# Ordering the first batch of an attention and mixer kernel by hand

## The chip, the cores and the metric

The kernel runs on one core of one Trainium2 chip. The time is device microseconds of one execution; medians of several executions are quoted. An execution counts as disturbed only when it is over 1.5% above the fastest of the same kernel. A trace and its page come from one execution with the profiler on, so a page shows one case of what varies between executions.

Names used below: PE is TensorE's matmuls, PEld its weight loads, DVE VectorE, ACT ScalarE, POOL GpSimd, SP SyncE. `SPq`, `ACTq`, `POOLq` mark what an engine's sequencer does, such as issuing a transfer.

## The reference

Eight batches; per batch twelve heads of cosine attention (448 rows, 64 columns), then a low-rank mixing over the rows, then two channel matmuls with a relu between, plus residual.

```python
q_n = q / (norm(q) + 1e-6);  k_n = k / (norm(k) + 1e-6)
attn = softmax(q_n @ k_n.T / tau)
x = concat_heads(attn @ v)                      # (8, 448, 768)
u = x + (x.T @ U @ V).T                         # rank 32, over the 448 rows
out = u + relu(u @ w_ch1) @ w_ch2               # 768 -> 3072 -> 768
```

## The kernel before

Heads are worked in pairs, six pairs to a batch, and pairs are loaded and normalised in groups (1, 1, 2, 2 pairs in the first batch, then 2, 2, 2). For a group: squares of queries and keys, their sums (`reduce`), a root on ScalarE (`root`), the inverse, and the scaling. For a pair: `step_T` transposes on TensorE and copies the result, `step_S` makes the scores and their exponentials, `step_V` the attention output in two halves, `step_A` and `step_H` the mixing, which ends in a copy into `u`. From the second batch on, TensorE is filled up between these steps with the channel matmuls of the batch before (`fill`). In the first batch there are none yet. The cuts below are shortened; `...` marks what is left out, and the last list is written with short names.

```python
def square(self, j):
    ...
    if self.early:                               # early = gi < 2 : groups 0 and 1
        nc.scalar.activation(sq[...], self.flat(t), AF.Square)
    else:
        nc.gpsimd.tensor_mul(sq[...], self.flat(t), self.flat(t))
...
def step_T(b, p):
    tp = psum.tile([128, 8, 128], BF, name="tp", tag="ps_x", bufs=1)
    ...                                          # eight transposes
    nc.vector.tensor_copy(out=t..., in_=tp...)   # qkT
...
def step_H(b, p):
    ...
    nc.vector.tensor_copy(out=u_of(b)[:, p, 0:S], in_=up)   # up: bank ps_x too
...
for n in range(NPAIR + 1):                       # one order for all batches (short names)
    parts = [S(n, 0, 1), V(n-1, 0), S(n, 2, 3), V(n-1, 1), T(n+1), A(n-1), H(n-1)]
    ...                                          # with shares of fill between
```

## Time and profile before

| | before |
|---|---|
| median time | 648.8 us |
| span of the profiled execution | 646.9 us |
| PE busy | 94% |
| first transposes | 13.06 us |
| first channel matmul | 62.43 us |
| TensorE full from | 64.6 us to 642.4 us |

The prediction below shows the page, the stretches and the chain; here is only how to read them. A row of digits has forty slices of 16 us, a 9 is a slice at least nine tenths busy. TensorE's row is full from the fifth slice, so this kernel can gain only in the first 65 us. One view is added here: stretches of the kernel before around its one clock dip. The columns are the stretch, its length, busy us and count of PE, PEld, DVE, ACT and POOL, the granted clock, the DMA share and GB/s.

```profile
46.00:49.60 3.60, 1.84 (x27) 1.15 (x23) 3.49 (x8) 1.15 (x4) 2.34 (x3) 1.00 1.15 234
49.60:56.50 6.90, 5.96 (x56) 3.83 (x52) 4.47 (x9) 3.32 (x5) 6.90 (x6) 0.51 1.14 231
```

TensorE was busy for half of the 3.6 us, and its granted clock is at half for the 6.9 us after them.

### The profile page before, as it was taken

The numbers are of one execution on the slowest core, as the hardware profiler recorded it, in microseconds if no ns is written. First come the engines' busy times: TensorE is split into PE (matmuls) and PEld (weight loads), VectorE is DVE, ScalarE is ACT, GpSimd is POOL, SyncE is SP. The second block draws the span as 40 slices with busy tenths as digits, with TensorE's granted clock in tenths as the row PEclk, the third lists the DMA queues.
The fourth block names the chain that finished last, engine by engine and source line by source line (L and its number), as shares of the span: only waits on it lengthen the run. The fifth ranks groups of instructions, "written<-read, shape, count | busy, mean of one in ns | idle before, by whom it ended". The sixth has DMA issues, their size and how long they took to land.

```text
span 646.9 us, 12173 instructions
## 1 busy us (share of the span) xinstructions
PE 609.4 (94%) x5160; PEld 360.4 (56%) x5160; DVE 273.3 (42%) x524; ACT 273.3 (42%) x501; POOL 195.2 (30%) x158
## 2 busy tenths in 40 slices
PE   1467999999999999999999999999999999999997
PEld 0244556655566556665566655665566555665564
DVE  4788335355244455364353453463442543210000
ACT  2465554345433454345433455334523454324310
POOL 7877244043141341340431431431404401000000
PEclk9997999999999999999999999999999999999999
DMA  7899991350315420161315302044311100001011
GB/s 195 196 220 234 233 241 43 98 147 4 83 35 126 110 73 16 32 168 48 86 26 135 95 24 79 25 117 105 87 25 26 50 1 1 25 25 26 1 50 49
DMA packets 51782, 54.33 MB, mean 84 GB/s; under 512 B 5552, under 2 KB 48112, under 8 KB 51728
## 3 DMA queue, kind: packets, MB, share of 16 engines
q1 hardware_dynamic: 44288, 43.14, 26.1%
q0 software_dynamic: 7120, 10.18, 8.6%
q8 instruction: 40, 0.66, 0.4%
q10 hardware_dynamic: 320, 0.23, 0.1%
q14 instruction: 14, 0.11, 0.1%
HBM read 52.02 MB, written 11.01 MB: 97 GB/s over the span
## 4 chain that ended last, share of the span: by engine, by line
PE 91%; DVE 6%; DMA 1%; ACT 0%; issue 0%; SPq 0%; ACTq 0%
PE mp L390 34%; PE mp L363 34%; PE av L309 5%; PE sc L282 5%; PE tp L260 3%; PE sc L274 2%; DVE qn L241 2%; PE av L302 2%; PE av L331 2%; DVE ss L215 1%; PE up L342 1%; PE mp L399 1%; PE up L347 1%; DVE qkT L262 1%; DVE X L316 1%; DMA kst<-in_k_dram 1%
## 5 line engine op out<-in xcount | busy, mean ns | idle before, releaser
L390 PE MATMUL mp<-w_sb,relu 128*128 128x384 bf16 x1344 | 246.8, 326 | 0.0
L390 PEld LDWEIGHTS <-relu 128*128 128x128 bf16 x1344 | 123.7, 98 | 77.9 <-issue 7.4
L241 POOL TENSOR_TENSOR kb<-kst,inv 128x512 bf16<-128x512 f32 x46 | 59.3, 1310 | 336.3 <-DVE inv L233 284.8
L363 PEld LDWEIGHTS <-w_sb 128*128 128x128 bf16 x1152 | 106.0, 98 | 92.9 <-issue 7.8
L284 ACT ACTIVATE E<-sc 128x896 bf16<-128x896 f32 x144 | 126.3, 917 | 46.3 <-PE sc L282 46.2
L367 ACT ACTIVATE relu<-mp 128x448 bf16<-128x448 f32 x156 | 84.7, 543 | 134.4 <-PE mp L363 134.4
L363 PE MATMUL mp<-uE,w_sb 128*128 128x448 bf16 x576 | 122.9, 353 | 1.1 <-DVE uE L349 1.1
L363 PE MATMUL mp<-uO,w_sb 128*128 128x448 bf16 x576 | 118.0, 353 | 0.0
L404 ACT COPY o_sb<-mp 128x384 f32<-128x384 f32 x50 | 23.9, 478 | 109.0 <-PE mp L399 109.0
L215 DVE TENSOR_REDUCE ss<-sq 128x16 f32<-128x1024 f32 (+1 forms) x50 | 58.1, 1166 | 3.3 <-ACT sq L207 3.3
L315 DVE RECIPROCAL rd<-av 128x4 f32<-128x4 f32 x96 | 17.1, 178 | 95.4 <-PE av L309 95.4
L241 DVE TENSOR_TENSOR qn<-qst,inv 128x512 bf16<-128x512 f32 x48 | 53.4, 1150 | 0.0
L282 PE MATMUL sc<-qkT 64*128 64x448 bf16 x288 | 45.5, 368 | 8.2 <-DVE qkT L262 6.1
L210 POOL TENSOR_TENSOR sq<-kst 128x1024 f32<-128x1024 f32 x23 | 52.0, 2262 | 2.7 <-DMA qst<-in_q_dram 2.7
L309 PE MATMUL av<-v,E 128*128 128x65 bf16 x1152 | 52.8, 195 | 0.0
L369 DVE TENSOR_SCALAR relu<-mp 128x448 bf16<-128x448 f32 x36 | 22.5, 625 | 67.0 <-PE mp L363 67.0
L262 DVE COPY qkT<-tp 128x1024 bf16<-128x1024 bf16 x48 | 33.0, 687 | 36.7 <-PE tp L260 36.7
L309 PEld LDWEIGHTS <-E 128*128 128x128 bf16 x1152 | 46.2, 98 | 0.0
L210 POOL TENSOR_TENSOR sq<-qst 128x1024 f32<-128x1024 f32 x23 | 43.5, 1892 | 0.0
L316 DVE TENSOR_TENSOR X<-av,rd 128x256 bf16<-128x256 f32 x96 | 40.8, 425 | 3.3
L334 ACT CAST A_sb<-av 128x128 bf16<-128x128 f32 x48 | 12.6, 263 | 61.7 <-PE av L331 61.7
L349 DVE CAST uO<-up 128x448 bf16<-128x448 f32 x24 | 14.9, 623 | 53.9 <-PE up L347 53.9
(66 smaller groups left out, 394.7 us busy)
## 6 DMA issues: line engine op xcount, KB each, us to landing
out_dram<-o_sb SPq DMA_DIRECT2D x54, 192.0 KB, 2.7
w_sb<-in_moe_w_ch_dram POOLq DMA_DIRECT2D x8, 1152.0 KB, 27.0
qst<-in_q_dram SPq DMA_DIRECT2D x23, 256.0 KB, 3.9
vst<-in_v_dram SPq DMA_DIRECT2D x46, 128.0 KB, 2.9
kst<-in_k_dram SPq DMA_DIRECT2D x44, 128.0 KB, 3.7
qst<-in_q_dram SPq DMA_DIRECT2D x23, 192.0 KB, 4.0
vst<-in_v_dram SPq DMA_DIRECT2D x46, 96.0 KB, 2.8
kst<-in_k_dram SPq DMA_DIRECT2D x44, 96.0 KB, 3.4
```

The lines of the kernel that those rows point to most:

```text
L210: nc.gpsimd.tensor_mul(sq[:, 0:self.nh * 4, :], self.flat(t), self.flat(t))
L215: nc.vector.reduce_sum(self.ss[:, j, 0:self.nh * 4], self.sq[j][:, 0:self.nh * 4, :], axis=AX.X)
L241: eng.tensor_mul(o[:, j, :, :, :], t[:, 2 * j:2 * j + 2, :, :].rearrange("p h c d -> p c h d"), iv.unsqueeze(3).to_broadcast([128, 4, 2, D]))
L262: nc.vector.tensor_copy(out=t.rearrange("p a b -> p (a b)"), in_=tp.rearrange("p a b -> p (a b)"))
L282: nc.tensor.matmul(out=sc[:, h, 0:S], lhsT=t[r, 1, c * 128:(c + 1) * 128], rhs=t[r, 0, 0:S], start=True, stop=True)
L284: nc.scalar.activation(out=e[:, 2 * c:2 * c + 2, 0:S], in_=sc[:, :, 0:S], func=AF.Exp)
L309: nc.tensor.matmul(out=av[:, i, h, :], lhsT=e[:, 2 * c + h, ic * 128:(ic + 1) * 128], rhs=vv[:, 2 * j + h, c, :], start=False, stop=(i == ...
L316: nc.vector.tensor_mul(X[:, 2 * half:2 * half + 2, :].rearrange("p i (h d) -> p i h d", h=2), av[:, :, :, 0:D], rd.rearrange("p (i h) o -> ...
L363: nc.tensor.matmul(out=mp, lhsT=w1_sb[:, cc, f * 128:(f + 1) * 128], rhs=u[:, cc, 0:S], start=(cc == 0), stop=(cc == CC - 1))
L367: nc.scalar.activation(out=relu[:, f, o:o + S], in_=mp, func=AF.Relu)
L390: nc.tensor.matmul(out=mp, lhsT=relu[:, f, r0:r0 + 128], rhs=w2_sb[:, f, half * HC:(half + 1) * HC], start=(f == 0), stop=False, skip_grou ...
L404: nc.scalar.copy(out=o[:, cols], in_=mp)
```

## The change

Its intent: the first batch has no channel matmuls to hide its waits, so its steps are written out by hand in the order in which the engines can take them, and work is moved off VectorE and GpSimd, which the first batch keeps busiest.

```diff
-        nc.gpsimd.dma_start(out=U_sb[0:64, :, 0:R], ...)       # mixer loads: POOL
+        nc.scalar.dma_start(out=V_raw, in_=moe_V)              # now ScalarE
+        nc.scalar.dma_start(out=U_raw[0:64, :, :], ...)
+        nc.scalar.dma_start(out=U_raw[64:128, 0:3, :], ...)
...
-            self.early = gi < 2
+            self.early = gi < 3                                # group 2's squares on ScalarE
...
+        if b == 0 and p < 2:                                   # qkT in halves
+            nc.scalar.copy(out=t[:, 1, :]..., in_=tp[:, 4:8, :])
+            nc.vector.tensor_copy(out=t[:, 0, :]..., in_=tp[:, 0:4, :])
...
+        if b == 0 and half == 1:                               # second half: channel bank
+            bank = psum.tile([128, 512], FP, name="mp", tag="ps_m", bufs=2)
...
+        if b == 0:
+            nc.scalar.copy(out=u_of(b)[:, p, 0:S], in_=up)     # u on ScalarE, also in ps_m
...
-    load(0, "k", nc.scalar)
-    load(0, "q", nc.sync)
+    load(0, "k", nc.sync, nc.scalar)                           # loads split over two queues
+    load(0, "q", nc.sync, nc.scalar)
...
+    A(3)                                                       # mixing one pair later
+    V(4, 0)
+    T(6)
+    Hs(3)
+    Sc(5, 2, 3)
+    V(4, 1)
+    g4.scale(0, 1, V_)
+    g4.values()
+    load_all(6)
+    load_w2(12, 24)                                            # fifth of five weight transfers
```

The hand order runs to pair 6's first scores; from there the loop with its fill goes on.

More of the change, by code (lines that the diff above doesn't have):

```diff
@@ L113 @@
     U_sb = const.tile([128, 4, 128], BF, name="U_sb")
-    V_raw = const.tile([R, S], BF, name="V_raw")
+    U_raw = const.tile([128, 4, R], FP, name="U_raw")
+    V_raw = const.tile([R, S], FP, name="V_raw")
     V_sb = const.tile([128, S], BF, name="V_sb")
@@ L123, in load_mixer @@
         nc.gpsimd.memset(U_sb, 0.0)
-        nc.gpsimd.dma_start(out=U_sb[0:64, :, 0:R],
-                            in_=moe_U[0:256].rearrange("(p c) r -> p c r", c=4))
-        nc.gpsimd.dma_start(out=U_sb[64:128, 0:3, 0:R],
-                            in_=moe_U[256:448].rearrange("(p c) r -> p c r", c=3))
         nc.gpsimd.memset(V_sb, 0.0)
-        nc.gpsimd.dma_start(out=V_raw, in_=moe_V)
+        nc.gpsimd.memset(U_raw[64:128, 3, :], 0.0)
+        nc.scalar.dma_start(out=V_raw, in_=moe_V)
+        nc.scalar.dma_start(out=U_raw[0:64, :, :], in_=moe_U[0:256].rearrange("(p c) r -> p c r", c=4))
+        nc.scalar.dma_start(out=U_raw[64:128, 0:3, :], in_=moe_U[256:448].rearrange("(p c) r -> p c r", c=3))
     def place_mixer():
@@ L134, in place_mixer @@
         body = V_sb[0:R, 0:384].rearrange("r (c p) -> r c p", p=128)
-        nc.gpsimd.tensor_copy(out=body[:, :, 0:64], in_=lo[:, 0:3, :])
-        nc.gpsimd.tensor_copy(out=body[:, :, 64:128], in_=hi)
-        nc.gpsimd.tensor_copy(out=V_sb[0:R, 384:448], in_=lo[:, 3, :])
+        nc.scalar.copy(out=U_sb[:, :, 0:R], in_=U_raw)
+        nc.scalar.copy(out=body[:, :, 0:64], in_=lo[:, 0:3, :])
+        nc.scalar.copy(out=body[:, :, 64:128], in_=hi)
+        nc.scalar.copy(out=V_sb[0:R, 384:448], in_=lo[:, 3, :])
     def load_w1(f0, f1):
@@ L159, with load @@
             group_of[(b, p0 + j)] = (gi, j)
-    def load(gi, what, eng):
+    def load(gi, what, *engs):
         b, p0, n = groups[gi]
+        engs = list(engs) * 4
         h0, nh = 2 * p0, 2 * n
@@ L174, in load @@
             allh = slice(h0, h0 + nh)
-            eng.dma_start(out=dst(qst[s], L, slice(0, nh), 4), in_=src(q, allh, 0, 256, 4))
-            eng.dma_start(out=dst(qst[s], U2, slice(0, nh), 3), in_=src(q, allh, 256, 448, 3))
+            engs[0].dma_start(out=dst(qst[s], L, slice(0, nh), 4), in_=src(q, allh, 0, 256, 4))
+            engs[1].dma_start(out=dst(qst[s], U2, slice(0, nh), 3), in_=src(q, allh, 256, 448, 3))
             return
@@ L179, in load @@
         ev, od = slice(h0, h0 + nh, 2), slice(h0 + 1, h0 + nh, 2)
-        eng.dma_start(out=dst(t, L, slice(0, nh, 2), 4), in_=src(x, ev, 0, 256, 4))
-        eng.dma_start(out=dst(t, U2, slice(0, nh, 2), 3), in_=src(x, ev, 256, 448, 3))
-        eng.dma_start(out=dst(t, L, slice(1, nh, 2), 3), in_=src(x, od, 0, 192, 3))
-        eng.dma_start(out=dst(t, U2, slice(1, nh, 2), 4), in_=src(x, od, 192, 448, 4))
+        engs[0].dma_start(out=dst(t, L, slice(0, nh, 2), 4), in_=src(x, ev, 0, 256, 4))
+        engs[1].dma_start(out=dst(t, U2, slice(0, nh, 2), 3), in_=src(x, ev, 256, 448, 3))
+        engs[2].dma_start(out=dst(t, L, slice(1, nh, 2), 3), in_=src(x, od, 0, 192, 3))
+        engs[3].dma_start(out=dst(t, U2, slice(1, nh, 2), 4), in_=src(x, od, 192, 448, 4))
     norm = {}
@@ L203, in square @@
             t = (qst, kst)[j][self.s]
-            sq = work.tile([128, NG * 4, D], FP, name="sq", tag="sq", bufs=2)
+            if self.gi < 2:
+                sq = work.tile([128, 8, D], FP, name="sq1", tag="sq1", bufs=2)
+            else:
+                sq = work.tile([128, NG * 4, D], FP, name="sq", tag="sq", bufs=2)
             self.sq[j] = sq
@@ L261, in step_T @@
         t = work.tile([128, 2, 512], BF, name="qkT", tag="qkT", bufs=3)
-        nc.vector.tensor_copy(out=t.rearrange("p a b -> p (a b)"),
-                              in_=tp.rearrange("p a b -> p (a b)"))
+        if b == 0 and p < 2:
+            nc.scalar.copy(out=t[:, 1, :].rearrange("p (c r) -> p c r", c=4), in_=tp[:, 4:8, :])
+            nc.vector.tensor_copy(out=t[:, 0, :].rearrange("p (c r) -> p c r", c=4), in_=tp[:, 0:4, :])
+        else:
+            nc.vector.tensor_copy(out=t.rearrange("p a b -> p (a b)"),
+                                  in_=tp.rearrange("p a b -> p (a b)"))
         qkT[(b, p)] = t
@@ L296, in step_V @@
         X = X_of[(b, p)]
-        bank = psum.tile([128, 512], FP, name="av", tag="ps_av", bufs=1)
+        if b == 0 and half == 1:
+            bank = psum.tile([128, 512], FP, name="mp", tag="ps_m", bufs=2)
+        else:
+            bank = psum.tile([128, 512], FP, name="av", tag="ps_av", bufs=1)
         av_of[(b, p)] = bank
@@ L337, in step_A @@
         est.act(0.3)
-        up = psum.tile([128, S], FP, name="up", tag="ps_x", bufs=1)
+        if b == 0:
+            up = psum.tile([128, S], FP, name="mp", tag="ps_m", bufs=2)
+        else:
+            up = psum.tile([128, S], FP, name="up", tag="ps_x", bufs=1)
         up_of[(b, p)] = up
@@ L348, in step_H @@
                          start=False, stop=True, skip_group_check=True)
-        nc.vector.tensor_copy(out=u_of(b)[:, p, 0:S], in_=up)
         est.pe(0.19)
-        est.dve(0.62)
+        if b == 0:
+            nc.scalar.copy(out=u_of(b)[:, p, 0:S], in_=up)
+        else:
+            nc.vector.tensor_copy(out=u_of(b)[:, p, 0:S], in_=up)
+            est.dve(0.62)
         if b % 2 == 1 and p == NP - 1:
@@ L440, in load_all, with T, Sc, V @@
                 load(gi, x, nc.sync)
-    load(0, "k", nc.scalar)
-    load(0, "q", nc.sync)
-    load(1, "q", nc.sync)
-    load(1, "k", nc.sync)
+    load(0, "k", nc.sync, nc.scalar)
+    load(0, "q", nc.sync, nc.scalar)
+    load(1, "k", nc.sync, nc.scalar)
+    load(1, "q", nc.sync, nc.scalar)
+    load(2, "k", nc.gpsimd)
+    load(2, "q", nc.sync)
     load(0, "v", nc.sync)
-    load(2, "q", nc.sync)
-    load(2, "k", nc.gpsimd)
     load(1, "v", nc.gpsimd)
+    load_mixer()
     load(2, "v", nc.sync)
-    g0, g1, g2, g3 = preps[0:4]
-    load_mixer()
+    g0, g1, g2, g3, g4 = preps[0:5]
+    V_, P_ = nc.vector, nc.gpsimd
+    def T(n):
+        step_T(*pairs[n])
+    def Sc(n, *cs):
+        step_S(*pairs[n], cs)
+    def V(n, half):
+        step_V(*pairs[n], half)
+    def A(n):
+        step_A(*pairs[n])
+    def Hs(n):
+        step_H(*pairs[n])
     g0.square(1)
     g0.square(0)
-    g1.square(1)
-    g1.square(0)
-    g2.square(1)
-    g2.square(0)
     g0.reduce(1)
@@ L463 @@
     g0.root()
+    g1.square(1)
+    g1.square(0)
     g0.invert()
-    g0.scale(1, 0, nc.vector)
-    g0.scale(0, 0, nc.vector)
-    g0.values()
-    place_mixer()
+    g0.scale(1, 0, V_)
+    g0.scale(0, 0, V_)
+    g2.square(1)
     g1.reduce(1)
-    step_T(*pairs[0])
+    T(0)
+    Sc(0, 0)
     g1.reduce(0)
     g1.root()
+    Sc(0, 1)
+    g2.square(0)
     g1.invert()
-    g1.values()
-    load_all(3)
+    g1.scale(1, 0, P_)
+    g1.scale(0, 0, V_)
+    g0.values()
+    load_all(3)
+    load_w1(0, 768)
+    T(1)
+    g2.reduce(1)
+    Sc(0, 2, 3)
+    g2.reduce(0)
+    g2.root()
+    Sc(1, 0, 1)
+    g2.invert()
+    g2.scale(1, 0, P_)
+    g2.scale(0, 0, V_)
+    g2.scale(1, 1, P_)
+    V(0, 0)
+    g1.values()
+    T(2)
+    place_mixer()
+    Sc(1, 2, 3)
+    V(0, 1)
+    g2.scale(0, 1, V_)
+    g3.square(1)
+    g3.square(0)
+    g2.values()
+    load_w1(768, 1920)
+    Sc(2, 0, 1)
+    load_all(4)
+    A(0)
+    V(1, 0)
+    T(3)
+    Hs(0)
+    Sc(2, 2, 3)
+    V(1, 1)
+    g3.reduce(1)
+    g3.reduce(0)
+    load_w1(1920, 3072)
+    Sc(3, 0)
+    g3.root()
+    Sc(3, 1)
+    g3.invert()
+    g3.scale(1, 0, P_)
+    g3.scale(0, 0, V_)
+    g3.scale(1, 1, P_)
+    A(1)
+    V(2, 0)
+    T(4)
+    g3.scale(0, 1, V_)
+    Hs(1)
+    Sc(3, 2, 3)
+    V(2, 1)
+    g3.values()
+    load_all(5)
+    g4.square(1)
+    g4.square(0)
+    Sc(4, 0, 1)
+    A(2)
+    V(3, 0)
+    T(5)
+    g4.reduce(1)
+    Hs(2)
+    Sc(4, 2, 3)
+    V(3, 1)
+    load_w2(0, 12)
+    g4.reduce(0)
+    Sc(5, 0)
+    g4.root()
+    Sc(5, 1)
+    g4.invert()
+    g4.scale(1, 0, P_)
+    g4.scale(0, 0, V_)
+    g4.scale(1, 1, P_)
+    A(3)
[8 more added lines that the diff above has]
+    load_w2(12, 24)
+    A(4)
+    V(5, 0)
+    V(5, 1)
+    Hs(4)
+    Sc(6, 0, 1)
+    A(5)
+    T(7)
+    Hs(5)
+    fill.extend(steps_m1(0) + steps_m2(0))
     after = {}
@@ L480, in put @@
         after.setdefault((n, at), []).append(fn)
-    for gi in range(1, len(groups)):
+    for gi in range(5, len(groups)):
         m, n, g = first_pair[gi], groups[gi][2], preps[gi]
         two = range(n)
-        if gi >= 3:
-            put(m - 3, 0, lambda g=g: (g.square(1), g.square(0)))
-            put(m - 3, 6, lambda g=g: g.values())
-        if gi == 2:
-            put(0, 0, lambda g=g: (g.reduce(1), g.reduce(0), g.root(), g.invert()))
-            put(0, 2, lambda g=g: ([g.scale(0, j, nc.vector) for j in two],
-                                   [g.scale(1, j, nc.gpsimd) for j in two], g.values()))
-        elif gi > 2:
-            put(m - 2, 0, lambda g=g: g.reduce(1))
-            put(m - 2, 1, lambda g=g: g.reduce(0))
-            put(m - 2, 2, lambda g=g: g.root())
-            put(m - 2, 3, lambda g=g: (g.invert(), [g.scale(1, j, nc.gpsimd) for j in two]))
-            for j in two:
-                put(m - 2, 4 + j, lambda g=g, j=j: g.scale(0, j, nc.vector))
-        if gi >= 1:
-            put(m - 1, 6, lambda gi=gi: load_all(gi + 3))
@@ L501 @@
-    put(0, -1, lambda: (g1.scale(1, 0, nc.vector), g1.scale(0, 0, nc.vector)))
-    put(1, 4, lambda: (load_w1(0, 768), load_w1(768, 1536)))
-    put(2, 4, lambda: (load_w1(1536, 2304), load_w1(2304, 3072)))
-    put(3, 4, lambda: (load_w2(0, 6), load_w2(6, 12)))
-    put(4, 4, lambda: (load_w2(12, 18), load_w2(18, 24)))
-    for n in range(NPAIR + 1):
+        put(max(m - 3, NP), 0, lambda g=g: (g.square(1), g.square(0)))
+        put(max(m - 3, NP), 6, lambda g=g: g.values())
+        put(m - 2, 0, lambda g=g: g.reduce(1))
@@ L508 @@
+        put(m - 2, 1, lambda g=g: g.reduce(0))
+        put(m - 2, 2, lambda g=g: g.root())
+        put(m - 2, 3, lambda g=g: (g.invert(), [g.scale(1, j, P_) for j in two]))
+        for j in two:
+            put(m - 2, 4 + j, lambda g=g, j=j: g.scale(0, j, V_))
+        put(m - 1, 6, lambda gi=gi: load_all(gi + 3))
+    put(NP, 6, lambda: load_all(7))
+    for n in range(NP, NPAIR + 1):
         b, p = pairs[n] if n < NPAIR else (B, 0)
-        prev = pairs[n - 1] if n > 0 else None
         now, nxt = n < NPAIR, n + 1 < NPAIR
-        parts = [
-            now and (lambda: step_S(b, p, (0, 1))),
-            prev and (lambda: step_V(*prev, 0)),
-            now and (lambda: step_S(b, p, (2, 3))),
-            prev and (lambda: step_V(*prev, 1)),
-            nxt and (lambda: step_T(*pairs[n + 1])),
-            prev and (lambda: step_A(*prev)),
-            prev and (lambda: step_H(*prev)),
-        ]
@@ L520 @@
-        weights = [w if part else 0 for part, w in zip(parts, (2, 2, 2, 2, 2, 2, 1))]
-        left = NP - p + 0.85 if p else 0.85
-        nf = len(fill) if p == 0 else int(round(len(fill) / left))
+        if n == NP:
+            parts = [None, None, lambda: Sc(n, 2, 3), None, None, None, None]
+        else:
+            parts = [
+                now and (lambda: Sc(n, 0, 1)),
+                lambda: V(n - 1, 0),
+                now and (lambda: Sc(n, 2, 3)),
+                lambda: V(n - 1, 1),
+                nxt and (lambda: T(n + 1)),
+                lambda: A(n - 1),
+                lambda: Hs(n - 1),
+            ]
@@ L523 @@
+        weights = [w if part or n == NP else 0 for part, w in zip(parts, (2, 2, 2, 2, 2, 2, 1))]
+        last = p == 0 and n > NP
+        left = NP - p + 0.85 if not last else 0.85
+        nf = len(fill) if last else int(round(len(fill) / left))
         given = acc = 0
-        for fn in after.pop((n, -1), []):
-            fn()
         for i, (fn, w) in enumerate(zip(parts, weights)):
@@ L535 @@
             given = want
-        if p == 0 and n > 0:
+        if last:
             while fill:
```

## The prediction

> **What bounds the kernel now.** I read the page first (busy shares and slices), then the stretches of the first batch, the chain that ended last, and the order of time on the engines.
>
> The page of the kernel before:
>
> ```profile
> PE 609.4 (94%) x5160; PEld 360.4 (56%) x5160; DVE 273.3 (42%) x524; ACT 273.3 (42%) x501; POOL 195.2 (30%) x158
> ...
> PE   1467999999999999999999999999999999999997
> ...
> PEclk9997999999999999999999999999999999999999
> DMA  7899991350315420161315302044311100001011
> ```
>
> From the fifth slice on TensorE is full until the tail. Only the first four slices, some 65 us, can be shortened; all later time is matmul work that the change does not touch. The stretches (us, then busy us and count of PE, PEld, DVE, ACT, POOL, then clock, DMA share, GB/s):
>
> ```profile
> 13.00:26.00 13.00, 4.09 (x23) 2.03 (x23) 11.17 (x16) 3.74 (x8) 9.24 (x9) 1.00 0.88 205
> 26.00:62.40 36.40, 26.39 (x316) 16.87 (x316) 28.35 (x56) 21.03 (x37) 28.76 (x25) 0.91 1.07 221
> ```
>
> While the first batch's attention runs, VectorE is busiest (39.5 of 49.4 us). The chain (start, length, what) agrees: it hops along VectorE's operations.
>
> ```profile
> 19.62 2.27 DVE ss L215 x2
> ...
> 23.25 2.15 DVE qn L241 x2
> ...
> 48.72 2.61 DVE qn L241 x2
> 51.33 0.54 DVE uE L349
> ...
> 64.61 0.35 PE mp L363
> ```
>
> The last line is the first channel matmul after which TensorE never waits again. So the figure to predict is when the changed kernel reaches the same state.
>
> The order of time at the start (start, us, engine; brackets: idle before):
>
> ```profile
> 3.65 0.49 ACTq L183 DMA_DIRECT2D kst<-in_k_dram  x1
> 6.99 0.63 ACT L207 ACTIVATE sq<-kst 128x512 f32<-128x512 f32 x1 [4.97 <-DMA kst<-in_k_dram]
> ...
> 9.68 0.63 ACT L207 ACTIVATE sq<-kst 128x512 f32<-128x512 f32 x1 [1.54 <-DMA kst<-in_k_dram]
> ...
> 10.73 0.20 ACT L224 ACTIVATE ss<-ss 128x16 f32<-128x16 f32 x1
> ...
> 15.59 1.89 POOL L210 TENSOR_TENSOR sq<-qst 128x1024 f32<-128x1024 f32 x1
> ...
> 16.18 1.32 DVE L231 TENSOR_SCALAR ss<-ss 128x16 f32<-128x16 f32 x1 [0.53 <-ACT ss L225]
> ```
>
> Group 0's root (10.73) stands behind group 1's squares, which wait for their load; its sums were ready at 9.1. And a VectorE operation of 0.17 us took 1.32 us: it ended at 17.50, with GpSimd's square (17.48).
>
> **What the Trainium skill says.** "SBUF — State Buffer", section "Who interferes with whom": VectorE and GpSimd share a port pair; an operation in a 2-port mode, or with two SBUF inputs, can block on the other; ScalarE never waits. The trace agrees (1.32 against 0.17 us; the query scaling took 0.68 us with GpSimd idle and 1.38 us beside its key scaling). "Trainium Kernel Development and Optimization", section "Key Constraints": issuing from several engines only saves the sequencer's issue time, the same 16 DMA engines serve all. Here an issue costs about 0.6 us, so that is what split loads can save. "TensorE: Matmul & The Clock Gate", Part 1: half clock until a window of about 3.4 us was busy. The trace agrees: four transposes took 0.61 us at 13 us and 0.38 us at 29 us, and the granted clock was 0.50 from 50 to 56 us, after two microseconds with TensorE half idle.
>
> **The change, part by part.** Durations are those of the trace above.
>
> Split loads: keys and queries of group 0 are issued in three slots per queue instead of four (one of them late, at 3.65), so group 0 lands near 5.5 us instead of 6.9. But the built order shows nine issues on ScalarE ahead of its first square, the last three for the mixer, and six of the nine carry a wait for an earlier transfer. The trace before shows eight transfers issued freely and the next waiting for a landing some 2.9 us after issue. SyncE issues group 1's first query transfer at about 4.1 us, it lands at 7.5; the mixer's last issue waits for it, 7.5 + 0.6 = 8.1. So the first square starts at 8.2, **1.2 us later** than now. The earlier root gains 1.6 us (10.73 against 9.15). Root at 10.35, first transposes at 12.7 against 13.05: only 0.4 us gained.
>
> Squares of group 2 on ScalarE: adds two of about 1.05 us there and removes 3.8 us of GpSimd; the 1.32 us block goes, and GpSimd scales group 1's keys beside VectorE. Group 2's sums, which hold up pair 1 now (19.6 to 23.25 in the chain), no longer stand before the first scaling of pair 1: its scores move from 26.1 to about 20.6, the largest single gain, 5.5 us.
>
> Evictions: six copies of u (0.62 us each) leave VectorE and become six of 0.54 us on ScalarE. Two query/key copies are halved: VectorE saves 0.3 us each, ScalarE gains 0.6 us each. Placing the mixer adds some 1.1 us to ScalarE.
>
> Mixing one pair later, and half of the attention output and u in the channel matmuls' banks: a transpose no longer waits for u's copy in its bank. Those waits are 3.0 us of TensorE in all now, but they lie on VectorE's time, not instead of it.
>
> Walking the new program order with these durations, each operation at the later of its engine being free and its inputs: scores of pair 2 start at 26.5 (31.4 now), of pair 3 at 30.7 (37.4), pair 4 at 38.5 (43.1), pair 5 at 43 (49.3), pair 6 at 52.5. VectorE then has an attention half every 2.9 us, 5.76 us a pair against 5.95 now. Its own work fell to about 4.9 us a pair (reduce 1.2, scaling 1.1, attention output 1.25, transposed copy 0.65, small ones 0.7), but it idles in each pair of groups: about 0.5 us for the round trip to ScalarE's root, and about 1.4 us for the attention output behind TensorE's transposes. ScalarE meanwhile waits 1.5 us with that root for the sums, and at the end copies pair 5's 128x128 block only after two exponentials of pair 6 (0.9 us each). That puts the last mixing at 55.1 and the first channel matmul at **55.3 us**.
>
> What compares with that: before, TensorE is full from 64.6, and its last matmul ends at 642.4. At that point it had done more than the changed kernel has at 55.3: the rest of pair 6's scores (0.59), half of pair 7's (0.48) and five channel matmuls (0.95), 2.0 us. So the equivalent time before is 62.6. Gain 62.6 - 55.3 = **7.3 us**. The tail and the 1.9 us between span and time stay. 648.8 - 7.3 = 641.5. I booked every query scaling at 1.1 us, and some of the second halves will find GpSimd idle at 0.7: I take 1 us off, **640.5 us**.
>
> Weights: no gain in itself. The DMA engines are full from 30 to 99 us now, and the eight transfers ran from issue at 31 to about 96:
>
> ```profile
> w_sb<-in_moe_w_ch_dram POOLq DMA_DIRECT2D x8, 1152.0 KB, 27.0
> ```
>
> That is 9.44 MB in 65 us, 145 GB/s. In the new order the first is issued at 19, the next two near 31, the last at 51: 1.2 MB land by 28, the other 8.3 MB 57 us after 31, at 88. The output matmuls start 36 us after the channel matmuls, at 91: 3 us to spare.
>
> **The rivals.**
>
> A: *the hand order closes most gaps.* VectorE's work from the first sum to pair 5's last output adds up to some 33 us; from 8.9 us, without any wait, that ends at 42, and channel matmuls could start near 45. For it: VectorE is the busiest engine before. Against: ScalarE has some 35 us of work from 8.2 on, equally full, and the two pass sums, roots and outputs back and forth. Half of the way would be 50: gain 12.6 us, 636.
>
> B: *the weights turn into the wait.* If the first phase shrinks a lot, output matmuls would start near 85 while the last weights land near 88 or later, since loads and weights want the same engines. That caps the gain at about 9 us: 640. For it: DMA share over 1 until 99 us. Against: fewer later groups compete by then.
>
> C: *TensorE stays at half clock.* It is full at half speed for about 6 us per pair (transposes 1.05, scores 2.0, outputs 2.1, mixing 1.2) against 3.1 at full speed. A dip or a late warm-up adds perhaps 2 to 4 us: 643 to 645. For it: the dip at 50 us now. Against: busier stretches come sooner.
>
> D: *ScalarE becomes the bound*, its blocked start and copies cancelling VectorE's relief: gain 3 us, 646.
>
> **Range and chances.** The walk carries about 4 us of error each way, mostly from waits between VectorE and ScalarE. Two per cent is 13 us, channel matmuls at 49.6; only rival A reaches it. So 634 to 646, and faster by over 2% with 0.2. Slower by 2% has no path that I see: 0.01.
>
> **What would show it.** First square at 8.2 us, after the mixer's issues; first transposes near 12.7; pair 1's scores near 20.6; no TENSOR_SCALAR of a microsecond on VectorE; first channel matmul near 55 with no TensorE wait after it; output matmuls near 91 without a wait for weights. Wrong: channel matmuls before 50 (the walk has too many waits), a wait of TensorE for a weight transfer (B), transposes at 0.6 us after 30 us (C), or ScalarE busy over 90% from 26 us on (D).

## The result, and the profile after

The median went from 648.79 to **647.27 us** (four executions each). The ratio of the means is 0.9976, 95% interval 0.9961 to 0.9991. A gain of 0.24% is there, but it is 1.5 us where 8.3 were predicted, and the time lies outside the range of 634 to 646.

The page after:

```profile
PE 613.3 (95%) x5160; PEld 363.6 (56%) x5160; DVE 271.3 (42%) x524; ACT 276.6 (43%) x508; POOL 187.7 (29%) x149
...
PE   1677999999999999999999999999999999999997
...
PEclk9977999999999999999999999999999999999999
```

TensorE's busy time rose by 3.9 us for the same 5160 matmuls, and the clock row has two slices at seven tenths where it had one. The stretches that answer to those of before:

```profile
13.00:26.00 13.00, 6.59 (x45) 3.28 (x43) 7.29 (x16) 8.13 (x16) 4.45 (x5) 1.00 0.80 184
26.00:61.50 35.50, 26.64 (x287) 18.50 (x288) 22.77 (x42) 20.31 (x37) 25.33 (x19) 0.81 1.12 232
```

VectorE's share did fall: from 39.5 us in the first batch to 30.1. It was relieved as planned, and the first batch hardly became shorter. The mean clock in the second stretch fell from 0.91 to 0.81. (The column does not show the slow start of the batch: it says 1.00 from 13 to 26 us, where four transposes took 0.61 us, against 0.39 at 60.89. The slow start is therefore read from durations.) Where the clock is low:

```profile
34.50:38.00 3.50, 0.85 (x21) 0.72 (x18) 2.84 (x6) 1.83 (x5) 0.40 (x1) 1.00 1.13 219
38.00:45.00 7.00, 6.27 (x58) 4.30 (x59) 3.44 (x9) 3.73 (x6) 7.00 (x5) 0.53 1.10 225
48.00:51.00 3.00, 0.99 (x22) 0.86 (x21) 2.34 (x6) 1.82 (x5) 0.58 (x1) 1.00 1.11 233
51.50:58.50 7.00, 5.75 (x60) 4.21 (x59) 4.43 (x5) 2.11 (x4) 6.98 (x6) 0.54 1.12 229
```

Twice TensorE is busy for only a quarter to a third of 3 us or more, and each time seven microseconds at half clock follow. Both gaps are the same step of the algorithm: TensorE waits for a group's sums, root, inverse and scaling before it can transpose. The prediction's own sign for its rival C, transposes at 0.6 us after 30 us, is there: 0.61 us at 39.14.

The order of time at the start and around the second dip (start, length, engine; in brackets the idle time before it and what ended it):

```profile
7.73 0.47 ACTq L129 DMA_DIRECT2D U_raw<-in_moe_U_dram  x1
8.31 0.63 ACT L212 ACTIVATE sq<-kst 128x512 f32<-128x512 f32 x1 [6.30 <-DMA kst<-in_k_dram]
...
13.91 0.58 ACT L268 COPY qkT<-tp 128x512 bf16<-128x512 bf16 x1 [0.97 <-PE tp L265]
...
14.53 0.42 DVE L269 COPY qkT<-tp 128x512 bf16<-128x512 bf16 x1 [1.15 <-ACT qkT L268]
...
55.01 1.91 POOL L215 TENSOR_TENSOR sq<-kst 128x1024 f32<-128x1024 f32 x1
...
55.39 3.93 DVE L246 TENSOR_TENSOR qn<-qst,inv 128x512 bf16<-128x512 f32 x1
...
56.87 1.89 POOL L215 TENSOR_TENSOR sq<-qst 128x1024 f32<-128x1024 f32 x1
```

Three things are to be seen. The first square follows the last mixer issue on ScalarE, at 8.31. The two halves of a copy run one after the other: VectorE's half starts when ScalarE's has ended. And one query scaling of VectorE, between 0.69 and 1.23 us elsewhere in the first batch, took 3.93 us: it started 0.4 us after GpSimd's square of the keys and ended 0.6 us after the next square, of the queries, had ended. Pair 5's outputs stood behind it on VectorE. The chain of the kernel after shows it, and then the full TensorE:

```profile
55.47 3.85 DVE qn L246
...
60.47 0.38 PE mp L343 x4
...
61.69 2.27 PE mp L381 x12
```

In the order of time the first channel matmul starts at 61.52, not at 55.3:

```profile
12.84 0.61 PE L265 MATMUL tp<-ident,qn 128*128 128x128 bf16 x4 [12.84 <-DVE qn L246]
...
61.52 2.43 PE L381 MATMUL mp<-uE,w_sb 128*128 128x448 bf16 x12
```

### The profile page after: what moved, and what is told of

Same layout as the page of the kernel before. It is cut to its first block, busy times and chain, and to the rows that moved or that the text cites. A ratio compares the mean times of both kernels' runs of the same rounds, so it can differ in the third digit from the quotient of the medians.

```text
span 645.7 us, 12177 instructions
## 1 busy us (share of the span) xinstructions
PE 613.3 (95%) x5160; PEld 363.6 (56%) x5160; DVE 271.3 (42%) x524; ACT 276.6 (43%) x508; POOL 187.7 (29%) x149
## 4 chain that ended last, share of the span: by engine, by line
PE 92%; DMA 3%; DVE 1%; SPq 1%; issue 1%; POOL 1%; ACT 0%; ACTq 0%; POOLq 0%
PE mp L408 34%; PE mp L381 34%; PE sc L291 5%; PE av L321 5%; PE tp L265 3%; PE sc L283 2%; DMA kst<-in_k_dram 2%; PE av L314 2%; PE mp L417 1%; PE av L343 1%; PE up L357 1%; PE up L362 1%; DMA qst<-in_q_dram 1%; DVE qn L246 1%; POOL kb L246 0%
## 5 line engine op out<-in xcount | busy, mean ns | idle before, releaser
L246 POOL TENSOR_TENSOR kb<-kst,inv 128x512 bf16<-128x512 f32 x47 | 60.8, 1314 | 344.3 <-DVE inv L238 324.0
L385 ACT ACTIVATE relu<-mp 128x448 bf16<-128x448 f32 x150 | 81.5, 543 | 133.2 <-PE mp L381 133.2
L387 DVE TENSOR_SCALAR relu<-mp 128x448 bf16<-128x448 f32 x42 | 26.2, 625 | 76.0 <-PE mp L381 76.0
L215 POOL TENSOR_TENSOR sq<-kst 128x1024 f32<-128x1024 f32 x22 | 50.1, 2276 | 0.0
L321 PE MATMUL av<-v,E 128*128 128x65 bf16 x1080 | 49.8, 195 | 0.0
L291 PE MATMUL sc<-qkT 64*128 64x448 bf16 x288 | 46.8, 374 | 2.5 <-ACT E L293 1.2
L321 PEld LDWEIGHTS <-E 128*128 128x128 bf16 x1152 | 47.7, 100 | 0.0
L215 POOL TENSOR_TENSOR sq<-qst 128x1024 f32<-128x1024 f32 x22 | 42.0, 1910 | 0.0
L265 PE MATMUL tp<-ident,qn 128*128 128x128 bf16 x192 | 19.7, 228 | 22.0 <-DVE qn L246 22.0
L328 DVE TENSOR_TENSOR X<-av,rd 128x256 bf16<-128x256 f32 x90 | 38.2, 425 | 3.1
```

The source lines that it names most:

```text
L215: nc.gpsimd.tensor_mul(sq[:, 0:self.nh * 4, :], self.flat(t), self.flat(t))
L246: eng.tensor_mul(o[:, j, :, :, :], t[:, 2 * j:2 * j + 2, :, :].rearrange("p h c d -> p c h d"), iv.unsqueeze(3).to_broadcast([128, 4, 2, D]))
L265: nc.tensor.transpose(out=tp[:, 4 * i + c, :], in_=t[:, j, c, :, :], identity=ident)
L291: nc.tensor.matmul(out=sc[:, h, 0:S], lhsT=t[r, 1, c * 128:(c + 1) * 128], rhs=t[r, 0, 0:S], start=True, stop=True)
L321: nc.tensor.matmul(out=av[:, i, h, :], lhsT=e[:, 2 * c + h, ic * 128:(ic + 1) * 128], rhs=vv[:, 2 * j + h, c, :], start=False, stop=(i == ...
L328: nc.vector.tensor_mul(X[:, 2 * half:2 * half + 2, :].rearrange("p i (h d) -> p i h d", h=2), av[:, :, :, 0:D], rd.rearrange("p (i h) o -> ...
```

## The experiments

By the walk I mean the prediction's timing of the new program order, operation by operation. My theory after reading this: the walk's order of events was right, and two things that it left out or had at the wrong size ate the gain, TensorE at half clock and the scaling beside GpSimd's squares (below: the collision). The rivals: waits that the walk took rightly but too short (loads, ScalarE's turn), or parts of the change that did nothing.

Executions of one variant spread by up to 6 us, and their start differs by 1 to 2 us with the landing of the first loads, so besides the medians I give **first transposes to first channel matmul** of the profiled execution, which leaves the start out. It is one execution's figure, and it leaves out what the clock does after the first channel matmul, so a difference of a microsecond in it shows nothing. The changed kernel has 61.5 - 12.8 = 48.7 us there; the walk had 55.3 - 12.7 = 42.6. The runs of before beside each group had a median of 648.65 to 649.0 us. All variants gave correct results.

### The changed kernel again

No edit.

> The changed kernel itself, unaltered, so that it shares chip and rounds with the others of this call. Expected 647.3 us as on record, with a spread of a microsecond or two between executions like the other variants showed, the shorter ones with the higher mean clock.

647.31 us (644.59 to 647.91, six executions), ratio 0.9972 (0.9957 to 0.9987). The result stands, and one execution in six was 2.7 us shorter than the median. The profiled one had the collision again (3.86 us), and 60.26 - 12.85 = 47.4, with TensorE at 0.50 clock from 60.3 to 63.7 us, in its first channel matmuls. So this measure differs by 1.3 us between two executions of one kernel.

### The collision alone

```diff
     T(6)
+    g4.scale(0, 1, V_)
     Hs(3)
     Sc(5, 2, 3)
     V(4, 1)
-    g4.scale(0, 1, V_)
```

> The changed kernel (647.3 us), with group 4's second query scaling moved on VectorE from behind pair 4's last attention half to right behind the transposes of pair 6, so that it no longer meets GpSimd's two squares of group 5. Theory (a port conflict on the path): that scaling took 3.93 us instead of 0.7 to 1.2, pair 5's outputs stood behind it, so the first channel matmul comes about 2.5 to 3 us sooner and the time is near 644.5. Rival (pair 5 is held by ScalarE's exponentials or by TensorE anyway): under 0.7 us, 646.6 or more.

645.81 us (644.41 to 647.90), ratio 0.9954 (0.9939 to 0.9969). The scaling took 1.24 us, but first transposes to channel matmul was 61.95 - 14.35 = 47.6, no shorter than in the second profile of the changed kernel (47.4): TensorE was still at 0.66 clock from 50 to 60 us. The executions fall in two kinds, 644.4 to 645.2 at a mean clock of 0.992 and 646.5 to 647.9 at 0.989. The first is what the theory expected, the second is near the rival. The gain of 1.5 us by the medians is not clear of noise (the intervals of this run and of the changed kernel overlap, and one of six executions of the unaltered changed kernel reached 644.59 too), so this run alone does not show that the collision is part of the cause.

### Copies whole again

```diff
-        if b == 0 and p < 2:
+        if False:
```

> The changed kernel with the transposed queries and keys of pairs 0 and 1 copied whole by VectorE again. The built order shows that VectorE's half waits for ScalarE's half, so the halves run one after the other (0.58 + 0.42 us against 0.69 whole), and VectorE idled 2.24 us before pair 1's half. Theory (the split costs): first scores about 0.35 us sooner, pair 1's some 0.7, the time about 1 us shorter, 646.3. Rival (author's intent, the split relieves VectorE): 0.3 to 0.6 us longer.

646.29 us (645.38 to 647.81), ratio 0.9964 (0.9952 to 0.9976): a microsecond shorter by the medians, as expected, but the intervals overlap, so this alone is not shown. The trace shows the mechanism: pair 1's whole copy starts 0.6 us after the last four of its transposes have started (19.48 and 18.84), without waiting for ScalarE. The collision was there (3.87 us).

### Mixer loads off ScalarE

```diff
-        nc.scalar.dma_start(out=V_raw, in_=moe_V)
+        nc.sync.dma_start(out=V_raw, in_=moe_V)       # and both parts of U
```

> The changed kernel with the three mixer loads issued by SyncE instead of ScalarE. Theory (ScalarE's issues with their waits block the first square): first square near 5.9 us instead of 8.3, first transposes near 10.5 instead of 12.8, and with what follows being a chain, 1.5 to 2.4 us shorter, near 645.3. Rival (a later wait, group 2's or group 3's loads or the clock, takes its place): first square earlier but the time within 0.5 us of the changed kernel.

645.37 us (642.46 to 647.71), ratio 0.9940 (0.9916 to 0.9965). First transposes at 11.29 instead of 12.84: the block on ScalarE was real, 1.55 us instead of the 2.3 expected. The executions spread by 5 us again, with the two shortest (642.5 and 642.7) at the highest clock, 0.995. In the profiled one there was no collision (0.68 us; GpSimd's squares came at 55.40, two microseconds after the scaling), yet 59.28 - 11.29 = 48.0, with the clock at 0.53 from 50 to 60 us.

### Keeping TensorE busy while it waits

Matmuls of constant tiles into a bank whose content is never read, put ahead of a pair's transposes, where TensorE waits anyway:

```diff
         qn, kb, _ = norm[gi]
+        extra = {0: 40, 1: 8, 2: 8, 4: 8, 6: 8}.get(b * NP + p, 0)
+        if extra:
+            wt = psum.tile([128, 512], FP, name="wt", tag="ps_x", bufs=1)
+            for _ in range(extra):
+                nc.tensor.matmul(out=wt[:, 0:448]..., lhsT=ident, rhs=E[0][:, :, S:512],
+                                 start=True, stop=True)
```

> The changed kernel plus idle-time matmuls without use (128x448, results never read) ahead of the transposes of pair 0 (40 of them) and of pairs 1, 2, 4 and 6 (8 each), while TensorE waits there for scaled queries. Theory (half clock costs): granted clock 1.0 and short matmuls from 13 to 62 us; transposes, scores and outputs that stand between VectorE's operations shorten, 2 to 3 us in all, near 644.8. Rival (TensorE's speed does not matter before the channel matmuls, VectorE and its waits set the pace): within 0.6 us of the changed kernel, or longer where the extra matmuls stand in the way.

**642.60 us** (641.44 to 643.35), ratio 0.9903 (0.9890 to 0.9915), with 72 matmuls more than the changed kernel. First transposes to channel matmul: 55.99 - 13.07 = 42.9 us, within 0.3 us of the walk. First transposes, the scaling, the first channel matmul, and stretches of this run:

```profile
13.07 0.38 PE L270 MATMUL tp<-ident,qn 128*128 128x128 bf16 x4
...
51.48 0.68 DVE L246 TENSOR_TENSOR qn<-qst,inv 128x512 bf16<-128x512 f32 x1
...
55.99 2.43 PE L386 MATMUL mp<-uE,w_sb 128*128 128x448 bf16 x12
...
38.00:45.00 7.00, 6.45 (x73) 4.49 (x72) 5.10 (x11) 5.80 (x10) 6.39 (x5) 0.76 1.11 232
...
51.50:58.50 7.00, 5.99 (x72) 3.82 (x71) 2.90 (x8) 3.82 (x9) 3.01 (x3) 1.00 1.12 230
```

The second dip is gone, the first is shortened. And the collision did not happen: with quicker transposes and outputs, VectorE had done the scaling (0.68 us, at 51.48) before GpSimd reached the squares (56.16). This one edit removed both, more than I had expected of it. What the clock is worth without the collision is seen against the early scaling above, which had none in its profile either: 645.81 to 642.60 is 3.2 us, and the intervals are apart. No run raised the clock in another way, so that the extra matmuls helped by the clock rests on the durations: twelve output matmuls take 0.54 us at full clock and 0.86 at half.

### Which half of the extra matmuls

> The changed kernel plus extra matmuls ahead of the transposes of pairs 4 and 6 only (8 each), to see which half-clock stretch costs. Theory (the two late dips, 38 to 45 and 51 to 58 us, with the query scaling that meets GpSimd's squares in the second): nearly the whole gain of the full set, 643.3 us. Rival (the cold start up to 31 us costs most): 646.

With those of pairs 4 and 6 only, four of six executions took 642.9 to 643.4 and two 647.2 and 648.8; median 643.37, ratio 0.9927 (0.9907 to 0.9947). The profile fell on the longest:

```profile
53.93 5.02 DVE L246 TENSOR_TENSOR qn<-qst,inv 128x512 bf16<-128x512 f32 x1
54.65 1.91 POOL L215 TENSOR_TENSOR sq<-kst 128x1024 f32<-128x1024 f32 x1
56.50 1.89 POOL L215 TENSOR_TENSOR sq<-qst 128x1024 f32<-128x1024 f32 x1
```

Here the clock is full while it happens (1.00 from 53.9 to 58.95), so a low clock is not needed for the collision: the scaling takes 4.3 us more than its 0.69, and 61.16 - 14.24 = 46.9. TensorE, idle meanwhile, then does its first channel matmuls at 0.50 clock (61.3 to 64.6 us). So a collision can bring a dip about; that a dip makes the collision likelier is suggested by the run before, but not shown. This execution was 5.4 us above the run's median; the other long one was not profiled.

> The changed kernel plus extra matmuls ahead of pairs 0, 1 and 2 only, the complement of the late set. If the half clock of the first 31 us costs on its own, TensorE's steps between VectorE's get about 1.5 us shorter by pair 3, and the time falls to 645.8 or, in executions where the second query scaling of group 4 then comes before GpSimd's squares, to 643. If only the late dips cost, 647.3 with the usual spread.

With those of pairs 0, 1 and 2 only: 644.81 us (643.06 to 645.64), ratio 0.9937 (0.9924 to 0.9949), and 58.85 - 13.13 = 45.7. There was no collision in the profile (0.68 us), and the clock was at 0.56 from 50 to 60 us. The late set gave nearly the whole gain in four of six executions, as its theory said, but the late dips are not all: the start set alone is 2.5 us shorter than the changed kernel, with intervals apart. How much of this is the slow start itself is not shown: against the early scaling, also without a collision, it is 1.0 us, and those intervals overlap.

### Both at once

The early scaling, with the extra matmuls of pairs 4 and 6:

> The changed kernel with the early query scaling and the extra matmuls of pairs 4 and 6 only. The kernel with the late extra matmuls alone had four executions at 642.9 to 643.4 and two at 647.2 and 648.8; in the slow profiled one the scaling took 5.0 us beside GpSimd's squares. Theory (port conflict, hit or missed by a small shift, is those 4 to 5 us): every execution at 642.5 to 644.5. Rival (the slow ones come from a late start or the clock): one or two of six still at 646 or more.

643.82 us; four executions of 643.5 to 644.3 and one of 645.9, ratio 0.9930 (0.9917 to 0.9943). The second kind of executions is gone but for that one, which stands above my band and is not explained. First transposes to channel matmul, from the profiled executions:

| | scaling as changed | scaling early |
|---|---|---|
| no extra matmuls | 48.7, 47.4 (both with the collision) | 47.6 |
| extra at pairs 4, 6 | 46.9 (with the collision) | 57.86 - 13.56 = 44.3 |

While TensorE is slow, taking the collision away changes nothing that these profiles show; once it is kept fast late, the collision is worth 2.6 us of this measure. That fits lost times which lie beside each other and partly hide one another, but each cell is one or two executions. By the medians the two edits do not add up to more than their parts: 1.5 us for the early scaling, 3.9 for the extra matmuls, where four of six executions, by their times, escaped the collision, and 3.5 for both. With the extra matmuls at the start too, 42.9 are reached.

### Undoing two parts of the change

The six copies of u back on VectorE:

```diff
-            nc.scalar.copy(out=u_of(b)[:, p, 0:S], in_=up)
+            nc.vector.tensor_copy(out=u_of(b)[:, p, 0:S], in_=up)
```

> The changed kernel with the six copies of u back on VectorE (0.62 us each there, 0.54 on ScalarE): undoes one part. Theory (moving them relieved the busiest engine): 1 to 2 us longer, 648.5 or more. Rival (VectorE idles enough in this order): within 0.6 us of 647.3, or faster.

648.78 us (647.48 to 649.69), ratio 0.9995 (0.9983 to 1.0007): moving them was worth about 1.5 us by the medians, though the intervals overlap a little.

Group 2's squares back on GpSimd:

```diff
-            self.early = gi < 3
+            self.early = gi < 2
```

> The changed kernel with group 2's squares back on GpSimd (two of 1.9 us there, two of 1.05 us off ScalarE): undoes one part. GpSimd idles from 9 to 17.5 us in the changed kernel, so the squares fit, but they meet VectorE's key and query scalings of group 0 at 11.5 to 12.8 us. Theory (port conflict): the first transposes 0.7 to 1.9 us later, the time 0.5 to 1.5 us longer. Rival (ScalarE is the tighter engine at the start): 0.5 us or more shorter.

649.82 us (648.24 to 651.86), ratio 1.0015 (1.0002 to 1.0027): 2.5 us longer, more than I expected. Two operations on VectorE at the start collide instead:

```profile
10.96 1.30 DVE L236 TENSOR_SCALAR ss<-ss 128x16 f32<-128x16 f32 x1 [0.53 <-ACT ss L230]
...
13.19 2.38 DVE L246 TENSOR_TENSOR qn<-qst,inv 128x512 bf16<-128x512 f32 x1
```

These take 0.17 and 0.69 us in the changed kernel. GpSimd's squares ran beside them (10.34 to 12.24 and 12.61 to 15.03), and first transposes come at 15.63, 2.8 us later. From there on nothing is lost: pair 1's scores start 8.33 us after the first transposes in both kernels, and 63.56 - 15.63 = 47.9. It is the same kind of collision as in the kernel before (1.32 us at 16.18), met at another place.

### Putting it together

Early scaling, whole copies and the mixer loads on SyncE, without extra matmuls:

> Three edits at once: second query scaling of group 4 early, whole copies on VectorE, mixer loads from SyncE; no extra matmuls. Theory (three separate losses on one chain): the medians' gains of 1.5, 1.0 and 1.9 us add up, 643 us. Rival (they share one wait, mostly the clock, which falls to half in the same stretches): about the best single one, 645.

643.82 us (643.18 to 644.31), ratio 0.9924 (0.9912 to 0.9936): 3.5 us off the changed kernel's 647.31, and the executions spread by 1.1 us only. The three single gains sum to 4.4.

The same with the extra matmuls:

> The three edits plus the extra matmuls ahead of the transposes of pairs 0, 1, 2, 4 and 6. With the extra matmuls alone the first channel matmul started at 56.0 us; the three edits take 2.0 (start) and 0.7 (copies) off: 53.3. But that run then lost some 1.4 us in the channel matmuls, waiting for ScalarE, whose root of group 5 waits for GpSimd's squares, and this grows when the squares do not come sooner. Theory (clock, then that wait): 640.5 us. Rival (group 5's loads set the pace: the squares waited for them): no better than 642.

642.96 us (642.09 to 646.23), ratio 0.9917 (0.9900 to 0.9935). This missed: it is no better than the extra matmuls alone, as the rival said. The channel matmuls started at 55.21 and then waited 1.3 us for an eviction on ScalarE, which stood behind group 5's root, which waited for GpSimd's squares, which waited for group 5's keys.

Two more edits for these waits:

```diff
     Hs(4)
-    Sc(6, 0, 1)
     A(5)
     T(7)
     Hs(5)
+    Sc(6, 0, 1)
...
-        put(m - 2, 0, lambda g=g: g.reduce(1))      # root, inverse, scalings likewise
+        o = 2 if gi == 5 else 0
+        put(m - 2, o, lambda g=g: g.reduce(1))
```

> The three edits and the extra matmuls, and two more for the waits that the last profile shows: pair 6's first scores go behind pair 5's mixing, so that ScalarE copies pair 5's block before pair 6's exponentials (0.8 us of TensorE), and group 5's sums, root and scalings go two to three steps later, so that ScalarE's root does not stand before the channel matmuls' evictions (1.3 us). Theory (these waits are what is left): 641 us. Rival (group 5's loads, which come late while the weights use the DMA engines, make a wait elsewhere): no better than 642.5.

**641.45 us** (640.68 to 643.70), ratio 0.9895 (0.9880 to 0.9911): the best median, 1.05% below the kernel before. The channel matmuls start at 53.87. Then group 5 stops it:

```profile
57.23 1.88 POOL L215 TENSOR_TENSOR sq<-kst 128x1024 f32<-128x1024 f32 x1 [7.48 <-DMA kst<-in_k_dram]
...
63.45 1.74 PE L386 MATMUL mp<-uE,w_sb 128*128 128x448 bf16 x6 [2.00 <-ACT relu L390]
```

One of the transfers of group 5's keys took 19.9 us to land in this trace. It was issued at 37.1, behind two weight transfers (from 31.6), and two more were issued before it landed (41.6 and 48.7). After the wait TensorE was at 0.50 clock from 64.2 to 67.5 us. So one more: the third transfer of the first weights behind group 5's load, and the root two steps later.

> The best kernel so far (641.45 us) with two edits for what its profile shows: group 5's key load took 19.9 us to land behind three weight transfers, so the third of the first weights is issued after group 5's load instead of with the second; and group 5's root goes two steps later still, so that ScalarE's evictions do not wait for it (2.0 us of TensorE). Theory (that wait is all that is left after 53.9 us): 639.5 us. Rival (the weights land late in return, and the output matmuls wait): no better than 641.5.

641.88 us (640.07 to 643.10), ratio 0.9886 (0.9870 to 0.9901): no better. GpSimd's squares came at 51.0 and the wait for an eviction fell from 2.0 to 0.7 us, but the channel matmuls started at 56.26: the squares now ran during pair 5's outputs, and TensorE's clock fell to 0.83 between 50 and 60 us. The wait for the load was taken away, and the time did not follow. Why pair 5 came later in this trace I did not test.

## Why the prediction was wrong

**Right: what bounds the time, and where the gain counts.** In the changed kernel TensorE is full from the first channel matmuls on. The four variants that start these earliest wait 0.7 to 2.0 us for an eviction after that. The gain is how much sooner they start.

**Right: the start.** First square predicted at 8.2, measured 8.31; first transposes 12.7 and 12.84; the mixer's issues on ScalarE as the cause, shown by moving them (11.29). Pair 1's scores came at 21.17, predicted 20.6, and no TENSOR_SCALAR of a microsecond is left on VectorE there. But what the prediction called the largest single gain, group 2's squares on ScalarE, did not act as it said: with them back on GpSimd pair 1's scores came no later after the first transposes (8.33 us), and what was lost was lost before these. The new order of group 2's sums, which that run keeps, is what remains as the reason.

**Right: the weights.** Output matmuls waited for no transfer. They started at 98.0, later than predicted because the channel matmuls did.

**The step that failed: rival C was set aside.** The walk's 55.3 us has no dip of the clock in it; the prediction put that rival away with "Against: busier stretches come sooner." The order that the walk made leaves TensorE idle around every group's root, deeper than before (busy 24% and 33% of the gaps, 51% before), and there were two dips of seven microseconds (0.53 and 0.54) instead of one. Rival C's own size, "perhaps 2 to 4 us", fits what the clock was worth without the collision (3.2 us by the medians); with the collision that the extra matmuls also removed it was 4.7, and the walk's 42.6 us were met at 42.9. What the prediction did not see is that a dip and a collision come on top of each other.

**Wrong in sign: "some of the second halves will find GpSimd idle at 0.7: I take 1 us off".** The three second halves of groups 2 to 4 took 0.86, 1.23 and 3.93 us; the last one found GpSimd at its squares. I had cited the very rule and applied it to the first group only. In the new order only a copy and a weight issue stand on GpSimd between group 4's scalings and group 5's squares, which the built order of both engines would have shown. Removing the collision alone gave 1.5 us by the medians, which is within noise.

**Missed: the halved copies.** I booked a saving of 0.3 us each on VectorE. VectorE's half waits for ScalarE's in the built order, and they ran in series. Undoing them gave 1.0 us by the medians, within the noise of two runs.

**The sum.** From the predicted 640.5 to the measured 647.3 are 6.8 us. By the medians they split into the 1.0 taken off wrongly, 1.1 that even the kernel with all extra matmuls keeps (642.6 against 641.5), 3.2 of clock and 1.5 of collision; as the last two overlap, another order of edits would divide them otherwise. The 1.1 is in part a wait that I had not looked for past the first channel matmul: in that kernel's profiled execution (643.2 us) the first channel matmul came at 55.99, 0.7 us after the walk's, and TensorE then waited 1.1 us for an eviction behind group 5's root.

Rival A, that hand order closes most gaps, was not seen: the kernel with the best median starts its channel matmuls at 53.9. Rival D was not seen either: ScalarE was busy 20.3 of 35.5 us.

## What to carry to other kernels

When a stretch is a chain across several engines, find out first at what clock TensorE runs in it, and count its busy share in windows of 3 to 4 us: an order that gathers waits in one place can cost more there than it saves. For each VectorE operation with two inputs in SBUF, look at what GpSimd will be doing at that moment in the new order, not in the old one, since a delay of a microsecond or two can decide whether they meet. And follow the first engine that is to be full for some microseconds beyond the point where it becomes full.

## What the Trainium skill lacked or had wrong

- "TensorE: Matmul & The Clock Gate", the closing table's advice against TensorE-idle gaps of more than about 3 us: dips also came without such a gap. (The same page's section "A second HAM failure mode: psum-queue depth-cycling" names frequent short idle spells as another cause, but gives no size.) The longest single wait before the dip at 38 us was 2.88 us, with TensorE busy 0.85 of 3.5 us; before the dip at 49.6 us of the kernel before no wait was over 1.02 us, with TensorE busy 1.84 of 3.6 us. So the busy share of the stretch counted, and not one gap alone. Where the limit lies is not shown: after 17.6 to 21.0 us of the kernel with all edits and the extra matmuls, busy 2.10 of 3.4 us, the clock was 0.50, and after 51.2 to 54.6 us of the early scaling with extra matmuls, busy 1.98 of 3.4 us, it stayed at 1.00.
- "SBUF — State Buffer", section "Who interferes with whom": it says who blocks whom for an instruction, but not that one VectorE instruction can be held over two GpSimd instructions that follow each other. Here a scaling of 0.69 us took 3.93 and 5.02 us and ended only after both squares (1.91 and 1.89 us) had. In the second case its record even starts 0.7 us before the first square's (53.93 and 54.65), though spans on GpSimd are rough.
- "Trainium Kernel Development and Optimization", section "Key Constraints": that queues share the 16 DMA engines and interleave agrees, but no size is given for what this does to a small load. A key transfer of group 5 (19.9 us) landed that late beside weight transfers, where the median of 128 KB key transfers was 3.7 us over the kernel before and 8.4 in its first 105 us, with its weights on the way.
